# Nyström attention and a squared-ReLU feed-forward layer on one core: the order table searched anew, with other costs for late loads, adding transfers and GpSimd's additions

## The chip, the core and the metric

The kernel runs on one core of a Trainium2 chip. A core has five instruction queues that run side by side: TensorE (PE), VectorE (DVE), ScalarE (ACT), GpSimd (POOL) and SyncE (SP), and 16 DMA engines that carry transfers between the chip's memory and the core. Each queue works in order, so an instruction that waits holds all that stand behind it on its queue. The metric is the time of one execution in microseconds (us) of device time, as the median of several runs.

## What is computed

Two layers stand behind one another. The attention has 8 batches of 8 heads, 576 tokens and 64 features a head, with 32 landmarks (means of 18 neighbouring tokens); the feed-forward layer has 4608 tokens, 512 inputs and 2048 hidden units.

```python
q_lm = q.reshape(B, H, m, S // m, D).mean(axis=3)      # m = 32 landmarks
k_lm = k.reshape(B, H, m, S // m, D).mean(axis=3)
A, Bm, C = sm(q, k_lm), sm(q_lm, k_lm), sm(q_lm, k)    # softmax of the scaled products
Z = Bm.T / (norm1(Bm) * norminf(Bm) + 1e-6)
for _ in range(6):
    Z = 2 * Z - Z @ Bm @ Z
attn = A @ Z @ C @ v
x = attn.transpose(0, 2, 1, 3).reshape(B * S, H * D)
out = (np.maximum(x @ w_in, 0) ** 2) @ w_out           # float32
```

## The kernel before

The eight batches go through the core one behind another, and the stages of neighbouring batches are interleaved so that TensorE always has matrix products to do. Each piece of work is an *op* with a name; a number behind the name is the batch. The ops that matter here are, in the order in which one batch needs them:

- `ldq`, `ldk`, `ldv`: transfers of q, k and v, cast to bf16 on the way, issued on GpSimd's queue (L429, L455). `lx3` to `lx5` load q and k of batches 3 to 5 a second time in another layout, into the tile `XS` (L435).
- landmarks: matmuls of the loaded tile for batches 0 to 5 (`lm`, L500 from `XS`). For batches 6 and 7 the sums over tokens come from *adding transfers* (`la`, L443): for each of q and k of each of the two batches, three transfers go to the same 384 KB of `XS`, which is free again once the landmarks of batch 5 are done (`lm5`). The first of the three writes, the other two add (`accum_op`), and each of these has to wait until the one before it has landed. `la6.12` is batch 6, k, the third. Two additions of halves follow for each batch (`lma6.0` for q, `lma6.1` for k, L510), then two more (`lmc`, L514), a scaling (`lme`) and a transpose (`lmt`).
- `T` (L484): transposes of q and k on VectorE. `B`, `Bmx` to `Brn`: the 32 by 32 softmax and its column sums; `Bad` (L670) is a tiny addition in that chain, `Brn` its reciprocal. `N` and `U`: the six steps of Z on TensorE and VectorE, with `bd` (L679) laying out the next step's factor. `SS`: scores of A and C in two halves, `SS4.0` and `SS4.1` for batch 4. `At`, `Amx`, `Asb`, `Aex`, `Asu`, `Arc`, `Aml`, `Ab`: the softmax of A, and `Cmx`, `Cex`, `Crc`, `Cnr`, `CT`: that of C. `CV`, `Zm`, `ZC` and `W`: the products that fold v, Z and w_in into one weight for the batch (`We`).
- `F` (L1111): the first feed-forward product, `R` (L1132 on ScalarE, L1134 on VectorE) its ReLU out of PSUM, `Q` (L1139, L1141) the square into the tile `G`. `O` (L1158): the second product, `Oe` its copy out of PSUM, `St` its store. `F`, `R` and `Q` of batch 0 and 1 work on tokens in two parts.

What stands where is not left to a scheduler at run time. A table of words, `ORDER`, lists all ops. A word gives the op, the PSUM bank after `@` and, after `/`, the engine (A, D or P) where it isn't the op's first. A planner walks the table with a duration for each op and a rate for the transfers, and each engine's queue then gets its ops by the planned starts. The planner's numbers thus decide nothing on the chip but the order. Those that the change touches are the rate of late transfers in bytes per us (`RATE["late"]`, L205), the weight of an adding transfer's bytes (`ADD_COST`, L1254) and GpSimd's times for `lma` and `lmc` (L510, L514). A pair of lines of the planner says that ops marked with `port` on VectorE and GpSimd follow one another:

```python
            if e in o.port:
                t = max(t, port)
```

GpSimd has eight semaphores for its transfers, used in turn, so that a ninth is issued only when the one eight places ahead has landed.

Of the kernel before, what the change touches and what calls it, by code (L numbers as in the profile page):

```python
# [265 lines left out]
def kernel(  # L266
# [207 lines left out]
    def attention(b):  # L474
# [32 lines left out]
        def landmarks_added():  # L507
            acc, ls, kS = ACC[i2], LS[:, 0, 0:256].rearrange("p (t r d) -> p t r d", t=2, d=D), ("LS", 0)
            for t in range(2):
                op(f"lma{b}.{t}", {"POOL": 0.9, "DVE": v_(384)}, lambda e, t=t: eng(e).tensor_tensor(  # L510
                    acc[:, t, :, 0:3], acc[:, t, :, 0:3], acc[:, t, :, 3:6], ALU.add),
                   R=[("ACC", i2, t)], W=[("ACC", i2, t)], port=("POOL", "DVE"))
# [783 lines left out]
Aml1.1/P lmc2.00 O1.2 U1.4 lmc2.01 Cex1.0 lme2.0 O0.2 lmt2.0 T2.00 lx3.0 B2@2 N1.5@5 O1.3 Bmx2
U1.5 Crc1 Bsb2 CT1.0 Bex2 O3.2 ldq5.0 Bsu2 Cmk1 Oe1.0 Brc2 CT1.1 Bml2 Ap1.1@6 St1 Btf2 ldk3.1
Btr2/A Bcs2 Zd1@3 CR1@1 Bct2 Ab1.1/A O3.3 bt2/D Bnm2 Bad2 CRe1 Brn2 T2.11 BBT2@5 Zi2/P CV1@6,1
Oe3.0 ldv2.10 Zm1 St3 O0.3 Yi2 CVe1.1/A CVe1.0 bd2.0 T2.01 ZC1@7 Ap1.0@2 Oe0.0/D ZCe1.0 N2.0@1
O2.0@4 Ab1.0/A ZCe1.1/D St0 U2.0 ldk4.1 bd2.1/D W1.2@5 W1.0@0 W1.1@2 We1.00 We1.01/D N2.1@7 O2.1  # L1300
We1.1 ldk5.0 U2.1 We1.2/D W1.3@0 ldv3.10 O2.2 We1.3 bd2.2 T3.00 F1.4@2 F1.0@6 R1.4/D F1.2@0 R1.0
# [12 lines left out]
ldv5.00 U3.1 ZCe2.0 ZCe2.1/D bd3.2/D O8.1 Bsb4 Asb3.1 Bex4 Oe7.0 Amx3.0 N3.2@7 Aex3.1 W2.0@2 St7
W2.2@0 W2.3@4 We2.0 Bsu4 U3.2 O8.2 bd3.3/D We2.2/D We2.3 N3.3@7 W2.1@2 O8.3 We2.1 Asb3.0 F2.3@4
U3.3 Oe8.0 Crc3.0 F2.2@0 Cnr3.0 R2.3 Brc4 St8 F2.1@2 Bml4/P R2.2 Btf4 F2.0@6 Q2.3 R2.1 F2.5@4
Q2.2 St4 R2.0 F2.7@0 Q2.1 Asu3.1 F2.10@2 R2.5 F2.6@6 bd3.4/D R2.7 CT3.1 F2.9@4 Q2.5 R2.6 Q2.7
lm5.0@1 R2.9 Q2.0 Q2.6/A N3.4@0 F2.4@6 Q2.9 la6.00 U3.4 F2.13@4 R2.10 bd3.5/D CT3.0 O9.0@0 lme5.0
R2.13/D ldv5.10 R2.4 F2.14@2 la7.00 Q2.10 Aex3.0 N3.5@1 F2.11@4 U3.5 R2.14 F2.8@6 Zm3.2 Zm3.3
Zm3.0 R2.11 Arc3.1 O10.0@1 Q2.4 Q2.14/A Aml3.1 O10.1 R2.8 Asu3.0 Q2.8/A F2.15@2 lmt5.0 Arc3.0  # L1320
Q2.11/A CV3@4,6 Aml3.0 O9.1 Q2.13 CVe3.0/A CVe3.1/A Zm3.1 Ab3.0 R2.15 F2.12@4 T5.01 la6.10 ZC3@6
O9.2 R2.12 Q2.15 ZCe3.0/D Btr4/A la6.01 Q2.12/A O10.2 ZCe3.1/D bt4/D Bcs4 T4.00 W3.3@6 ldv6.11
W3.0@2 Ab3.1 W3.2@4 We3.0 We3.3/D O9.3 We3.2 O10.3 Oe9.0/D la7.10 BBT4@6 Bct4 F3.0@2 Oe10.0 Bnm4
F3.1@4 Bad4 Brn4 R3.0 T4.11 St10 Zi4/P O12.0@7 la7.01 R3.1 Yi4 bd4.0/D F3.2@0 T4.01 Q3.1/A St9
N4.0@6 W3.1@2 R3.2 U4.0 B5@4 O12.1 bd4.1/D We3.1 Bmx5 T5.00 N4.1@6 F3.3@0 Bsb5 Q3.2/A U4.1 O12.2
bd4.2 Bex5 R3.3/D Q3.0/A F3.6@4 Bsu5 la6.02 Brc5 T4.10 F3.5@0 N4.2@6 F3.4@2 Q3.3 R3.5 U4.2 la6.11
O12.3 R3.6 bd4.3/D Q3.5 R3.4 Bml5 N4.3@6 F3.9@0 Btf5 U4.3 Oe12.0 F3.7@4 Bcs5 bd4.4 R3.9/D F3.13@2
St12 la7.11 Bct5 F3.10@6 Q3.9/A R3.7/D N4.4@0 O11.0@1 R3.13 Q3.6 U4.4 R3.10 Bnm5 O11.1 T5.10
bd4.5 Q3.4/A SS4.0@2,4,6 Q3.7 Q3.10/A Bad5 N4.5@0 O11.2 la7.02 Brn5 Btr5 U4.5 At4.0 O11.3 bt5
Amx4.0 SS4.1@6 Zi5/P Oe11.0 ldv4.11 O13.0@0 Cmx4.1 St11 Cmx4.0 O15.0@1 Cex4.1 At4.1 O15.1 Cex4.0  # L1330
Asb4.0 BBT5@6 F3.12@4 Zm4.0 Aex4.0 Yi5 F3.11@2 Zm4.3 Crc4.1 Amx4.1 F3.8@6 R3.11 la6.12 Asu4.0
# [80 lines left out]
```

## Time and profile before

| | |
|---|---|
| median of 3 runs | 259.1 us (259.07 to 259.11) |
| the profiled execution | 259.34 us, of which 257.6 us from the first to the last instruction |
| granted TensorE clock | 0.999 |
| busy share of the span | PE 96%, DVE 82%, ACT 68%, POOL 33% |
| DMA: GpSimd's queue (q0) and the stores' (q1) | 58.7% and 14.0% of 16 engines' span |

The profiled execution is 0.24 us longer than the median. Its times are from the first instruction on. A busy PE is not PE at its peak, since matmuls overlap; a gap between two groups of matmuls shows as an idle time with the engine or the transfer that ended it. In a list of waits, each row gives who waited (engine, tile, line), for whom, and three numbers: us in all, times, longest. In a row of a timeline stand the start, the duration, engine, line, operation and tiles.

### The profile page before, as it was taken

What the parts mean: (1) busy time and instruction counts of PE and PEld (TensorE: products, weight loads), DVE (VectorE), ACT (ScalarE), POOL (GpSimd) and SP (SyncE); (2) the same over time, 40 slices, a digit from 0 to 9 for tenths busy, and PEclk for the clock granted to TensorE, in tenths of its full rate; (3) what the DMA queues carried; (4) which work ended last, traced back from release to release, by engine and by line L of the source; (5) the groups of instructions that cost most, each with busy time, mean ns of one, the idle gap of its engine ahead of it and who ended that gap; (6) DMA issues with size and microseconds to landing.
All of it is one profiled execution on the core that took longest, in us unless ns stands there. A gap on an engine that the chain in (4) does not pass through costs nothing.

```text
span 257.6 us, 7492 instructions
## 1 busy us (share of the span) xinstructions
PE 247.5 (96%) x3043; PEld 138.1 (54%) x3043; DVE 212.5 (82%) x553; ACT 175.6 (68%) x324; POOL 85.1 (33%) x137
## 2 busy tenths in 40 slices
PE   6999989999999989999999999999999999999993
PEld 2565554557464566565553565456454565467442
DVE  2989999889999988999999999987989698877201
ACT  0834876567697799788686699699865879457220
POOL 8576845652535304348561540110100300000000
PEclk9999999999999999999999999999999999999999
DMA  5999999999999999799979794032104110051035
GB/s 99 209 190 204 206 209 207 208 240 227 224 225 209 223 230 283 164 194 181 196 138 205 192 156 94 3 80 46 43 21 104 43 42 0 3 124 42 10 67 129
DMA packets 24610, 36.53 MB, mean 142 GB/s; under 512 B 2560, under 2 KB 13632, under 8 KB 24576
## 3 DMA queue, kind: packets, MB, share of 16 engines
q0 software_dynamic: 18656, 26.61, 58.7%
q1 hardware_dynamic: 5760, 9.31, 14.0%
q8 instruction: 24, 0.39, 0.6%
q10 hardware_dynamic: 160, 0.13, 0.2%
q14 instruction: 10, 0.08, 0.1%
HBM read 48.50 MB, written 9.44 MB: 225 GB/s over the span
## 4 chain that ended last, share of the span: by engine, by line
PE 66%; DMA 15%; DVE 10%; POOL 3%; issue 2%; ACT 2%; DVEq 0%; POOLq 0%
PE ps L1158 38%; PE ps L1111 16%; DMA X<-in_q_dram 9%; DMA XS<-in_q_dram 6%; PE ps L935 3%; DVE RS L1134 2%; PE ps L864 2%; DVE G L1141 2%; POOL X L429 1%; PE ps L778 1%; ACT WP L416 1%; DVE sm L816 1%; PE ps L529 1%; PE ps L742 1%; DVE An L1081 1%
## 5 line engine op out<-in xcount | busy, mean ns | idle before, releaser
L1158 PE MATMUL ps<-w_out,G 128*128 128x512 bf16 (+1 forms) x592 | 138.3, 374 | 0.3 <-DVE RS L1134 0.3
L1158 PEld LDWEIGHTS <-G 128*128 128x128 bf16 x592 | 53.2, 98 | 53.9 <-issue 6.0
L1111 PE MATMUL ps<-AT,WP 128*128 128x288 bf16 (+2 forms) x512 | 71.2, 286 | 1.1 <-DVE RS L1134 0.8
L1132 ACT ACTIVATE RS<-ps 128x576 bf16<-128x576 f32 (+2 forms) x101 | 61.1, 651 | 10.5 <-PE ps L1111 5.0
L1111 PEld LDWEIGHTS <-WP 128*128 128x128 bf16 x512 | 48.5, 98 | 20.6 <-issue 2.5
L1139 ACT ACTIVATE G<-RS 128x576 bf16<-128x576 bf16 (+2 forms) x55 | 36.4, 686 | 2.1 <-DVE RS L1134 1.8
L416 ACT COPY OS<-ps 128x512 f32<-128x512 f32 (+1 forms) x32 | 18.3, 573 | 23.0 <-PE ps L1158 21.8
L1141 DVE TENSOR_TENSOR G<-RS 128x576 bf16<-128x576 bf16 (+2 forms) x71 | 30.1, 445 | 2.6 <-ACT RS L1132 2.0
L416 ACT CAST WP<-ps 128x1024 bf16<-128x1024 f32 (+1 forms) x25 | 23.5, 983 | 6.7 <-PE ps L935 6.5
L679 POOL TENSOR_TENSOR BD<-ST,blkb 128x256 bf16<-128x256 bf16 x15 | 10.8, 718 | 47.4 <-DVE ST L756 43.2
L1134 DVE TENSOR_SCALAR RS<-ps 128x576 bf16<-128x576 f32 (+2 forms) x27 | 20.4, 760 | 4.9 <-PE ps L1111 3.8
L484 DVE STREAM_TRANSPOSE TT<-X 128x576 uint32<-128x576 uint32 x32 | 24.3, 761 | 0.0
L819 ACT ACTIVATE C<-ps,sm 128x576 bf16<-128x576 f32 x16 | 14.2, 902 | 7.7 <-DVE sm L816 7.7
L756 DVE SCALAR_TENSOR_TENSOR ST<-ST,ps 128x128 bf16<-128x128 bf16 (+1 forms) x48 | 12.8, 266 | 5.9 <-PE ps L742 3.6
L455 POOL DMA_DIRECT2D V<-in_v_dram x24 | 14.5, 603 | 6.2 <-DMA X<-in_q_dram 2.6
L420 DVE COPY OS<-ps 128x512 f32<-128x512 f32 x5 | 3.4, 675 | 12.3 <-PE ps L1158 12.3
L816 DVE TENSOR_REDUCE sm<-ps 128x1 f32<-128x576 f32 x16 | 11.5, 747 | 1.2 <-PE ps L778 1.1
L1236 PE MATMUL ps<-onesb 128*128 128x512 bf16 (+1 forms) x36 | 10.6, 392 | 1.6 <-DVE onesb L352 1.6
L420 DVE CAST WP<-ps 128x1024 bf16<-128x1024 f32 (+1 forms) x9 | 9.9, 1100 | 1.8 <-PE ps L935 1.7
L429 POOL DMA_DIRECT2D X<-in_q_dram x16 | 9.8, 642 | 4.1 <-PE ps L1111 2.2
L429 POOL DMA_DIRECT2D X<-in_k_dram x16 | 9.7, 607 | 3.6 <-DMA X<-in_k_dram 1.3
L1081 DVE TENSOR_TENSOR An<-SA,smA 128x640 bf16<-128x640 f32 (+1 forms) x12 | 10.3, 864 | 0.1
(151 smaller groups left out, 307.5 us busy)
## 6 DMA issues: line engine op xcount, KB each, us to landing
...
X<-in_k_dram POOLq DMA_DIRECT2D x16, 288.0 KB, 11.7
X<-in_q_dram POOLq DMA_DIRECT2D x16, 288.0 KB, 11.0
V<-in_v_dram POOLq DMA_DIRECT2D x8, 288.0 KB, 11.8
XS<-in_q_dram POOLq DMA_DIRECT2D x6, 384.0 KB, 6.5
XS<-in_k_dram POOLq DMA_DIRECT2D x6, 384.0 KB, 7.1
...
```

The costliest lines, as they stand in the source:

```text
L416: nc.scalar.copy(o, i)
L429: lambda e: nc.gpsimd.dma_start(x[:, t, r].rearrange("p s d -> p (s d)"), src),
L455: lambda e, r=r, p0=p0, n=n, src=src: nc.gpsimd.dma_start(vv[32 * p0:32 * (p0 + n), r].rearrange("p s d -> p (s d)"), src),
L484: op(f"T{b}.{t}{r}", {"DVE": v_(576) + 0.02}, lambda e, r=r: nc.vector.transpose(tt[:, t, r].rearrange("p s m e -> p (s m e)").bitcast(U32 ...
L816: op(f"Cmx{b}.{r}", {"DVE": v_(576)}, lambda e, r=r: nc.vector.tensor_reduce(s_[:, 12 + r:13 + r], cbanks(r), axis=AX.XY, op=ALU.max, nega ...
L819: op(f"Cex{b}.{r}", {"ACT": a_(576) + 0.27}, lambda e, r=r: nc.scalar.activation(Cs[r][:].rearrange("p x u -> p u x"), cbanks(r), AF.Exp, ...
L1111: nc.tensor.matmul(ps[:, ph.at + i, 0:w], lhsT=wp[:, r, 128 * ff:128 * ff + 128], rhs=at[:, r, t0:t0 + w], start=(r == 0), stop=(r == 1))
L1132: nc.scalar.activation(rs, pair(ph, w), AF.Relu)
L1134: nc.vector.tensor_scalar(out=rs, in0=pair(ph, w), scalar1=0.0, scalar2=None, op0=ALU.max)
L1139: nc.scalar.activation(g, rs, AF.Square)
L1141: eng(e).tensor_tensor(g, rs, rs, ALU.mult)
L1158: nc.tensor.matmul(bank(po)[:, 0:c1 - c0], lhsT=G[:, f, lo:lo + P], rhs=w_out[:, f, c0:c1], start=(f == 0), stop=(f == NF - 1))
```

## The change

Four numbers of the planner are set anew, and the table behind the shared beginning is another. The first 60 TensorE ops with the first rows of the other queues stay as they are, up to the column sums of batch 1's B (`Bcs1`) and some ops behind them; all that follows stands in another sequence, in part in other banks and on other engines. No product, sum or transfer is added or removed.

```diff
-RATE = {"sw": 0.375e6, "hw": 0.2e6, "first": 0.385e6, "then": 0.4e6, "late": 0.385e6}
+RATE = {"sw": 0.375e6, "hw": 0.2e6, "first": 0.385e6, "then": 0.4e6, "late": 0.355e6}
...
-                op(f"lma{b}.{t}", {"POOL": 0.9, "DVE": v_(384)}, lambda e, t=t: eng(e).tensor_tensor(
+                op(f"lma{b}.{t}", {"POOL": 1.5, "DVE": v_(384)}, lambda e, t=t: eng(e).tensor_tensor(
...
-                op(f"lmc{b}.0{j}", {"DVE": v_(256), "POOL": 0.65}, lambda e, j=j: eng(e).tensor_tensor(
+                op(f"lmc{b}.0{j}", {"DVE": v_(256), "POOL": 1.0}, lambda e, j=j: eng(e).tensor_tensor(
...
-ADD_COST = 1.5
+ADD_COST = 0.5
...
-R0.20/D R0.2 F0.18@4 R0.0 Q0.2 W0.2@6 Bad1 F0.22@2 R0.18/D We0.2 Q0.0/P F0.16@0 Brn1 R0.22/D
...
+R0.20/D R0.2 F0.18@4 R0.0 Q0.2 W0.2@6 Bad1 F0.22@2 R0.18/D We0.2 ldv1.00 F0.16@0 Brn1 R0.22/D c18
+Q0.0/A F0.12@4 F0.14@6 Zi1 Aex1.0 Btr1 R0.16/D O1.0@3 Q0.20/P Q0.22/A R0.14 BBT1@2 F0.30@0 Yi1
```

Of the table three lines are shown; the rest of it is told by the queues that come of it.

Three places of the queues matter most. In the rows below, a number behind a tile's name tells its buffers apart.

The first is GpSimd's queue just behind the shared beginning, before:

```order
L470 DMA w_out<-in_moe_w_out_dram 128x4x512 x2
L1141 TENSOR_TENSOR G<-RS_125 128x2x256
L455 DMA V_66<-in_v_dram 128x1152
L368 AFFINE_SELECT seg<-onesb 96x32
L370 AFFINE_SELECT seg<-seg 96x32
L455 DMA V_66<-in_v_dram 96x1152
```

and now:

```order
L470 DMA w_out<-in_moe_w_out_dram 128x4x512 x2
L455 DMA V_66<-in_v_dram 128x1152
L368 AFFINE_SELECT seg<-onesb 96x32
L370 AFFINE_SELECT seg<-seg 96x32
L1141 TENSOR_TENSOR G<-RS_127 128x2x320
L1141 TENSOR_TENSOR G<-RS_126 128x2x320
L429 DMA X_62<-in_k_dram 128x1152
L455 DMA V_66<-in_v_dram 96x1152
L1141 TENSOR_TENSOR G<-RS_128 128x2x320
L1141 TENSOR_TENSOR G<-RS_125 128x2x256
L1141 TENSOR_TENSOR G<-RS_126 128x2x256
```

The square `Q0.0`, the first L1141 of before, has gone to ScalarE's queue, and five other squares of batch 0 stand on GpSimd's (`Q0.20`, `Q0.18`, `Q0.30`, `Q0.8`, `Q0.10`) where `Q0.30` alone was left before; the ReLU `R0.16` goes from ScalarE to VectorE.

The second is GpSimd's queue where the adding transfers (L443) begin, before:

```order
L429 DMA X_63<-in_k_dram 128x1152
L429 DMA X_63<-in_q_dram 128x1152
L455 DMA V_67<-in_v_dram 128x1152
L619 TENSOR_TENSOR Bf_104<-Bl_102,sm_117 128x64
L443 DMA XS<-in_q_dram 128x2x384
L455 DMA V_67<-in_v_dram 96x1152
```

and now:

```order
L429 DMA X_63<-in_k_dram 128x1152
L429 DMA X_62<-in_q_dram 128x1152
L679 TENSOR_TENSOR BD_100<-ST_0_98,blkb 128x256
L679 TENSOR_TENSOR BD_101<-ST_1_99,blkb 128x256
L443 DMA XS<-in_q_dram 128x2x384 x2
L455 DMA V_67<-in_v_dram 32x1152
L443 DMA XS<-in_k_dram 128x2x384
```

Fewer loads are ahead of the first of them than before (35.96 MB as the table counts bytes, against 37.14 MB), and the loads of batch 5's second layout (`lx5`) stand further ahead, as the 32.42nd MB in place of the 34.78th. From there to the last adding transfer of batch 6, `la6.12`, the queue now holds `la6.00`, `la7.00`, a small part of v, `la6.10`, `la6.01`, `la6.11`, `la6.02`, `la7.10`, `ldk6.0`, `ldk5.1`, `la7.11`, `la7.01`, `ldk7.0`, `la7.12`, `ldq6.0` and `la6.12`: three first transfers of a sum ahead of the adding ones, and one among them; seven adding ones; four loads of q or k.

The third is VectorE's queue at batch 6's additions of halves (L510). Before, they stood behind batch 4's last step and its transposes (L1084), among the transposes of batches 5 and 6 (L484):

```order
L756 SCALAR_TENSOR_TENSOR ST_0_98<-ST_1_99,ps 128x128
L484 STREAM_TRANSPOSE TT_69<-X_64 128x576
L1084 STREAM_TRANSPOSE AT_81<-An_79 128x2x128
L679 TENSOR_TENSOR BD_100<-ST_0_98,blkb 128x256
L484 STREAM_TRANSPOSE TT_68<-X_62 128x576
L510 TENSOR_TENSOR XS<-XS 128x2x192
L420 CAST WP_94<-ps 128x2x512
```

Now the one of k, `lma6.1`, stands here:

```order
L703 TENSOR_TENSOR ST_0_98<-ps,sm_118 128x2x32
L679 TENSOR_TENSOR BD_100<-ST_0_98,blkb 128x256
L898 TENSOR_TENSOR ZM_86<-ST_0_96,blk_138 64x128
L816 TENSOR_REDUCE sm_117<-ps 128x1
L700 TENSOR_TENSOR ST_0_98<-Bf_105,sm_118 128x2x32
L1064 STREAM_TRANSPOSE SA_77<-ps 128x256 x2
L510 TENSOR_TENSOR XS<-XS 128x2x192
L830 RECIPROCAL sm_117<-sm_117 128x1
L422 TENSOR_SCALAR C_84<-C_84,sm_117 128x576
L756 SCALAR_TENSOR_TENSOR ST_1_99<-ST_0_98,ps 128x128
```

It has moved ahead, to the transposes of batch 4's second half of scores (L1064), and the row behind it with L756 is `U5.0`, the first step of Z for batch 5. The additions of batch 7, which stood on GpSimd, are on VectorE now: `lma7.1` right behind that `U5.0`, ahead of the layout `bd5.1` (L679) that batch 5's second step needs, and `lma7.0` later.

More of the change, by code (lines that the diff above doesn't have):

```diff
@@ L1296 @@
[L1296 to L1301, printed above, removed]
@@ L1314 @@
[L1314 to L1319, printed above, removed]
@@ L1320 @@
[L1320 to L1331, printed above, removed]
@@ new lines @@
+Cex4.0 Brn5 Yi5 bd5.0/D St10 Zm4.3 O13.0@1 Q3.13/A Cmx4.1 ldv5.10 Zi5 ldv5.00 Cex4.1 F3.11@2
+At4.1 St12 O13.1 ldq7.1 lma6.1/D R3.11 ldq7.0 Crc4.1 N5.0@6 Cnr4.1 F3.15@4 Q3.11/A U5.0 ldv6.00
+lma7.1/D F3.8@2 R3.15 bd5.1/D O14.0@7 CT4.1 R3.8 Asb4.0 N5.1@4 O14.1 Crc4.0 Q3.8 Aex4.0 Zm4.0
+F3.14@5 U5.1 bd5.2/D F3.12@2 Cnr4.0 R3.14 N5.2@4 O13.2 R3.12 U5.2 CT4.0 Q3.15/A O14.2 lmc6.00
+Zm4.2 Zm4.1 Q3.14/A Amx4.1 CV4@2,5 Q3.12/A Asb4.1 O15.2 CVe4.1 Aex4.1 Asu4.0 lmc6.01/P O15.3
+CVe4.0/A Arc4.0 Asu4.1 bd5.3 ZC4@5 O13.3 Oe15.0 ZCe4.0/D ldv7.11 lme6.0 ZCe4.1/D St15 N5.3@4
@@ L1377 @@
+O34.0@4 Q7.7 St30 Q7.13 O32.0@2 R7.11 R7.12/D Q7.11/A O35.5 F7.15@0 O35.6 R7.15/D O31.0@3 Q7.12
+O34.1 Q7.15 O34.2 O35.7 O31.1 Oe35.2 St35.4 O32.1 O32.2 O32.3 O31.2 Oe32.0 O34.3 St32 O31.3
+Oe34.0 O33.0@2 St34 Oe31.0 O33.1 St35.3 O33.2 St31 O33.3 O35.0@6 Oe33.0 O35.1 O35.2 St33 O35.3
+Oe35.0 St35.2 St35.1
 """
```

147 lines of the change are left out of this document (80 added, 67 removed).

## The prediction

> **What bounds the kernel now.** I read the busy shares first, then the list of TensorE's waits, then the timeline around the longest of them, and last the transfers. Shares and slices (a digit is the busy share of 6.4 us in tenths):
>
> ```profile
> PE 247.5 (96%) x3043; PEld 138.1 (54%) x3043; DVE 212.5 (82%) x553; ACT 175.6 (68%) x324; POOL 85.1 (33%) x137
> PE   6999989999999989999999999999999999999993
> DVE  2989999889999988999999999987989698877201
> DMA  5999999999999999799979794032104110051035
> ```
>
> TensorE works without a break from the first slice on; VectorE is nearly as full up to about 200 us, and the DMA engines are up to about 97 us. So the time is TensorE's work and the waits in it, and whatever is late on VectorE or in the transfers turns into such a wait. The waits of TensorE:
>
> ```profile
> PE ps L1236 <- DVE onesb L352: 1.6, 1, 1.6
> PE ps L1111 <- DVE RS L1134: 0.8, 1, 0.8
> PE ps L500 <- DMA XS<-in_q_dram: 0.7, 1, 0.7
> PE ps L1158 <- DVE RS L1134: 0.3, 1, 0.3
> PE ps L911 <- DVE CV L420: 0.2, 1, 0.2
> PE ps L911 <- DVE ZM L898: 0.2, 1, 0.2
> ```
>
> The first lies in the shared beginning. The other five, 2.2 us together, are what a new order can win in whole waits. The reader is to see how little that is: a change that moves nothing but the order has 1% of the time ahead of it, and a single new wait on VectorE can cost as much.
>
> **The first wait, 0.8 us, and Q0.0.** VectorE and GpSimd at that place, and the spread of line 670:
>
> ```profile
> 31.82 1.13 DVE L670 TENSOR_SCALAR sm<-sm 128x2 f32<-128x2 f32 x1
> 32.86 0.81 DVE L1134 TENSOR_SCALAR RS<-ps 128x640 bf16<-128x640 f32 x1
> 31.86 1.05 POOL L1141 TENSOR_TENSOR G<-RS 128x512 bf16<-128x512 bf16 x1
> L670 DVE TENSOR_SCALAR sm<-sm x7: 169/170/1131, 31.8 to 188.1; 128x2 f32<-128x2 f32 x7
> ```
>
> `Bad1` on two numbers takes 1.13 us in place of 0.17, for as long as GpSimd squares `Q0.0`; the ReLU behind it (`R0.18`) then frees a bank late, and `F0.12` waits. With `Q0.0` on ScalarE nothing on GpSimd stands beside `Bad1`, and 0.8 us goes. ScalarE pays one square, about 0.64 us, beside its 32% of idle time, and loses `R0.16` to VectorE (about 0.8 us); `F0.30`, which takes that bank, follows by TensorE's own work some 2.5 us behind `F0.16`, and VectorE's chain of two ReLUs, a transpose and `R0.16` just fills that, so 0 to 0.2 us is late next. I take −0.8 (bounds −0.95 and 0).
>
> Beside it: the Trainium skill, "SBUF — State Buffer", section "Who interferes with whom", says that VectorE and GpSimd share one pair of ports as an exclusive lock, held for the whole instruction. This row agrees (1.13 us against 0.17).
>
> Five squares of batch 0 stand on GpSimd now, where two did, and a square of 640 takes 1.27 us there:
>
> ```profile
> L1141 POOL TENSOR_TENSOR G<-RS x2: 1052/1158/1265, 31.9 to 39.8; 128x512 bf16<-128x512 bf16 x1, 128x640 bf16<-128x640 bf16 x1
> 135.40 0.99 DVE L898 TENSOR_TENSOR ZM<-ST,blk 64x128 bf16<-64x128 bf16 x1
> 134.79 1.51 POOL L510 TENSOR_TENSOR XS<-XS 128x384 f32<-128x384 f32 x1
> L898 DVE TENSOR_TENSOR ZM<-ST,blk x24: 202/220/994, 71.0 to 220.8; 64x128 bf16<-64x128 bf16 x24
> ```
>
> The last three rows are a second hold of the same kind: a `Zm` of 0.22 us takes 0.99 beside GpSimd's addition of halves, and gives the two waits of L911, 0.4 us. Those additions are on VectorE now (0.53 us each), so −0.4. Against it I set new holds: of two squares on GpSimd one cost TensorE 0.8 us, the other nothing; three more squares at 0.4 each would cost 1.2, but the table's `port` rule places most of them, so I take +0.4 (bounds 0 and +1.2). The wait of L1158, 0.3 us, comes of a like hold of a `Cnr` by a `bd`; such pairs are drawn anew, so it counts 0.
>
> **The landmarks of batch 5, 0.7 us.** The chain of work at that place, and the last loads ahead of the first adding transfers, by start:
>
> ```profile
> 80.79 15.54 DMA XS<-in_q_dram
> 96.46 0.84 PE ps L500 x24
> 84.64 0.59 POOL L429 DMA_DIRECT2D X<-in_k_dram  x1
> 87.44 0.53 POOL L455 DMA_DIRECT2D V<-in_v_dram  x1 [1.67 <-DMA X<-in_q_dram]
> ```
>
> and their times from issue to landing, in the same order of loads (k, then v):
>
> ```profile
> X<-in_k_dram POOLq DMA_DIRECT2D x1, 288.0 KB, 15.8
> V<-in_v_dram POOLq DMA_DIRECT2D x1, 288.0 KB, 16.0
> ```
>
> `lx5` lands at 80.79 + 15.54 = 96.3 us and `lm5` starts then. It now stands 2.36 MB further ahead in a queue that is never empty. The loads between (k at 84.64 + 15.8 = 100.4, a q, v at 87.44 + 16.0 = 103.4) land 1.5 us apart, 0.59 MB each, so that is 6 us sooner, at about 90, against a start of `lm5` at about 95. −0.7 (bounds −0.75 and 0).
>
> **The adding transfers, where a wait is new.** Their issues and landings:
>
> ```profile
> 97.61 0.75 POOL L443 DMA_DIRECT2D XS<-in_q_dram  x1 [4.96 <-PE ps L742]
> 112.18 1.23 POOL L443 DMA_DIRECT2D XS<-in_q_dram  x1 [0.96 <-issue]
> XS<-in_q_dram POOLq DMA_DIRECT2D x1, 384.0 KB, 5.8
> 123.70 1.25 POOL L443 DMA_DIRECT2D XS<-in_k_dram  x1
> XS<-in_k_dram POOLq DMA_DIRECT2D x1, 384.0 KB, 7.5
> q0 software_dynamic: 1587, 2.38, 96.2%
> ```
>
> The fourth and sixth rows' transfers are `la7.01` and `la6.12`: they land at 112.18 + 5.8 = 118.0 and 123.70 + 7.5 = 131.2. Between them stand four more adding transfers and a small part of v (0.4 us), so five land in 12.8 us: 2.56 us each, with GpSimd's queue alone taking 96% of the 16 engines from 117 to 132 us (the last row). A first transfer of a sum is cheap beside that: the one issued at 97.61 and the ones behind it land at 104.9 to 107.4, some 0.9 us each.
>
> Now the new queue. Its loads ahead of the first `la` end two loads sooner than those of before, at 103.4 − 2 × 1.5 = 100.4 us. Three first transfers and a small v: 3 × 0.9 + 0.4 = 3.1, so 103.5. From there to `la6.12`: seven adding ones at 2.56 (17.9), one first (0.9), four loads at 1.5 (6.0): it lands at 103.5 + 24.8 = 128.3 us. Before, it landed at 131.2, and nobody looked for it until 139.1 (the additions of halves).
>
> VectorE reaches `lma6.1` sooner than that. From the order and these rows:
>
> ```profile
> 124.11 1.42 DVE L816 TENSOR_REDUCE sm<-ps 128x1 f32<-128x576 f32 x2 [0.31 <-PE ps L778]
> 125.45 0.77 DVE L1064 STREAM_TRANSPOSE SA<-ps 128x256 f32<-128x256 f32 x2
> L510 DVE TENSOR_TENSOR XS<-XS x2: 517/532/548, 140.9 to 142.9; 128x384 f32<-128x384 f32 x2
> L510 DVEq EVENT_SEMAPHORE  x1: 21/21/21, 139.1 to 139.1; - x1
> ```
>
> The first row is what follows the second half of batch 4's scores, at 124.1. The same products of TensorE are ahead of it (0.2 us more), less 1.5 us of waits: 122.8. Behind it now stand two `Cmx` (0.71 each by the row), the pair of `At` (0.77), and between them `Bad5`, `Brn5`, `Yi5`, `bd5.0`, a `Zm` and `Zi5`, some 0.2 to 0.3 each, 1.4 together: `lma6.1` is due at 126.4 and stands until 128.3. Behind it are `Crc`, `Cnr`, `U5.0`, `lma7.1` and `bd5.1`, 2.4 us with its own 0.53, and then TensorE's `N5.1`, due by its own work 6.3 us behind the scores (five groups of four O at 0.86, three F at 0.49, some small ones), at 128.5. It starts at 130.7 in place of 128.5: +2.2. TensorE can do nothing else meanwhile, since its queue is in order. At an adding cost of 2.2 us the transfer lands at 125.8 and only 0.3 is left (VectorE's own length); with loads that end 2 us later the wait is 4.2. Bounds +0.3 and +4.2; I take 2.2, by the 2.56 of the fullest stretch. `la6.02` for `lma6.0` lands by the same count at 111.5, VectorE comes at 113: 0, by a margin of 1.5.
>
> In a sentence by itself: the Trainium skill, "DMA: Bandwidth & Descriptors", section "Anatomy of one DMA — SWDGE (gpsimd) path", fits a transfer at 2.0 us plus its bytes over 436e3 per us, which by its figures (an estimate) makes 0.9 us of an adding 384 KB in a full queue, so `la6.12` would land near 117 and the sum would be 2.2 us lower. The trace has 2.56 us, and I go by that.
>
> **The rest.** TensorE changes its tiling shape four times more behind the shared part (97 for 93); a group of four O ahead of such a change takes longer in the chain by 0.1 us, yet other short ops are saved one:
>
> ```profile
> 98.44 0.86 PE ps L1158 x4
> 103.80 0.97 PE ps L1158 x4
> ```
>
> +0.2 (bounds 0 and +0.4). Three two-input ops leave GpSimd and seven ops come to ScalarE, some 4.6 us beside 82 us of idle: 0; were that cover gone, a ReLU would be late by its 0.65. The loads of `lx3` and `lx4` land within 0.5 us of their landmarks, as before: 0 (up to +0.5 each). The end (the last O, its copy and two stores) has the same sequence: 0.
>
> **Sum.** 259.34 − 0.8 − 0.4 + 0.4 − 0.7 + 2.2 + 0.2 = 260.2 for the profiled execution; less the 0.24 by which it lies above the median, 260.0 us.
>
> **Rivals.** (a) The adding transfers are in time. Then the last step's own 0.3 is left of 2.2: 258.1, and with no new hold 257.7. For it speak the first transfers at 0.9 us and a lone adding transfer that lands within 5 us; against it the 96% of the engines. It decides at 2.2 us an adding transfer. The skill's fit above is a case of it. (b) A wide square on GpSimd holds VectorE in batch 0 and 1, with the wait of the adding transfers beside it: five squares at 1.05 to 1.27 us, each able to take up to 0.8 from TensorE; at three, +2.0 over the forecast: 262.0. For it speaks one hold in two squares, against it that VectorE's reads from PSUM (`R`, `U`, the reductions) ran at full speed beside the other. It decides when a `Q`, `Zi` or `bd` of VectorE falls under a square. (c) The gains are as told and the DVE wait is 1 us: 258.8, about no change.
>
> **How the numbers follow.** A measurement of this kernel tells 0.2% (0.5 us) from no change. Forecast (wait of about 2 us; 258.9 to 261.3): 0.45, of it 0.38 slower, 0.04 the same, 0.03 faster. (a), 256.6 to 258.5: 0.33, faster. (b), 261 to 264: 0.16, slower. (c): 0.06, of it 0.05 the same, 0.01 faster. Together faster 0.37, the same 0.09, slower 0.54. The range from 257.2 to 262.6 leaves out the lower end of (a), with no hold and no late load, and the upper end of (b).
>
> **What the profile of the changed kernel would show.** `Bad1` at 0.17 us and no wait at `F0.12`; L500 of batch 5 with no transfer ahead of it; a wait of VectorE's queue at L510 near 126 us for `XS` and one of TensorE at L742 or L747 of batch 5's second step near 128. Wrong would be: L510 without a wait, adding transfers that land 1 to 2 us apart, or a TensorE wait of over 1 us at a place that isn't named here.

## The result, and the profile after

The changed kernel takes 267.12 us (265.70 to 268.30) against 259.11 us before (259.07 to 259.61): a ratio of 1.030, with a 95% interval of 1.027 to 1.033. It is 3% slower, and it lies above the whole range that was forecast. Its profiled execution took 266.59 us, 7.25 us more than the one before. Ratios leave out an execution that lies more than 1.5% above the shortest of its kernel, which is one of run 1 and one of run 9. The kernel before was measured again beside the runs below (medians of 258.98 to 259.36 us), and their ratios are to that.

Busy shares and slices of the page after:

```profile
PE 249.8 (94%) x3043; PEld 138.1 (52%) x3043; DVE 209.0 (79%) x549; ACT 181.0 (68%) x331; POOL 83.8 (32%) x134
...
PE   6998999999999999998749999999999999999993
...
DVE  2988986898999999977367999989897988966200
...
PEclk9999999999999999999968999999999999999999
```

A slice is 6.6 us; PEld is TensorE's load of weights, and PEclk its granted clock in tenths. Up to 119 us TensorE's slices read much as before; then VectorE falls to 3 tenths and TensorE to 4, and TensorE's granted clock drops for two slices. TensorE's waits after:

```profile
PE ps L742 <- DVE BD L679: 5.0, 1, 5.0
...
PE ps L689 <- POOL BD L679: 1.4, 1, 1.4
...
PE ps L1158 <- DVE SA L1064: 0.4, 1, 0.4
...
PE ps L1111 <- ACT RS L1132: 0.3, 1, 0.3
```

The waits at L1111 for VectorE (0.8), at L500 (0.7) and the two at L911 (0.2 each) of before are not in the list any more. In their place stand 5.0 us at L742, batch 5's second step of Z (`N5.1`), and 1.4 us at L689, where the first step starts from `bt5` (`BBT5`).

The timeline around them: GpSimd's row of `bt5`, VectorE's rows from the scores' transposes to `bd5.1`, and TensorE's rows.

```profile
123.55 1.69 POOL L443 DMA_DIRECT2D XS<-in_k_dram  x1
124.30 1.64 POOL L679 TENSOR_TENSOR BD<-Bt,blkb 128x256 bf16<-128x256 bf16 x1
...
127.95 0.77 DVE L1064 STREAM_TRANSPOSE SA<-ps 128x256 f32<-128x256 f32 x2
134.26 0.56 DVE L510 TENSOR_TENSOR XS<-XS 128x384 f32<-128x384 f32 x1 [5.55 <-DMA XS<-in_k_dram]
...
135.88 0.28 DVE L679 TENSOR_TENSOR BD<-ST,blkb 128x256 bf16<-128x256 bf16 x1
...
125.99 0.21 PE L689 MATMUL ps<-Bt,BD 128*128 128x32 bf16 x2 [1.42 <-POOL BD L679]
...
136.22 0.29 PE L742 MATMUL ps<-ST,BD 128*128 128x64 bf16 x2 [5.03 <-DVE BD L679]
```

The reader is to see one chain: the first row issues the transfer `la6.12`; VectorE stands at L510 (`lma6.1`) for 5.55 us until it lands; `bd5.1` is behind that, and TensorE's `N5.1` behind `bd5.1`. Ahead of it, GpSimd does `bt5` only once it has issued `la6.12`, and takes 1.64 us for it.

Three windows of the same profile. Behind the stretch and its length stand the busy times of PE, PEld, DVE, ACT and POOL (with the number of instructions), then TensorE's granted clock, the DMA share (which can pass 1) and GB/s:

```profile
130.00:136.20 6.20, 1.20 (x7) 0.42 (x5) 1.90 (x7) 1.26 (x3) 1.59 (x3) 0.84 1.13 248
136.20:141.00 4.80, 4.78 (x19) 2.41 (x20) 3.11 (x11) 2.21 (x4) 0.00 (x0) 0.50 1.12 208
141.00:146.00 5.00, 5.00 (x98) 2.59 (x97) 4.84 (x11) 3.33 (x7) 1.92 (x3) 1.00 0.78 141
```

Behind the wait TensorE is busy for 4.78 of 4.80 us, but at half its clock: that loses 4.80 × 0.50 = 2.4 us. The balance of the profiled execution: 1.9 us of waits gone, 5.0 + 1.4 + 0.3 + 0.1 come, and 2.4 us of clock, together +7.3, against 7.25 measured.

### The profile page after: what moved, and what is told of

The parts are those of the page before. It is cut to its first block, busy times and chain, and to the rows that moved or that the text cites. A ratio compares the mean times of both kernels' runs of the same rounds, so it can differ in the third digit from the quotient of the medians.

```text
span 264.9 us, 7495 instructions
## 1 busy us (share of the span) xinstructions
PE 249.8 (94%) x3043; PEld 138.1 (52%) x3043; DVE 209.0 (79%) x549; ACT 181.0 (68%) x331; POOL 83.8 (32%) x134
## 4 chain that ended last, share of the span: by engine, by line
PE 69%; DMA 20%; POOL 5%; issue 3%; DVE 1%; ACT 1%; POOLq 0%
PE ps L1158 41%; PE ps L1111 18%; DMA XS<-in_k_dram 9%; DMA X<-in_q_dram 4%; DMA XS<-in_q_dram 4%; DMA w_out<-in_moe_w_out_dram 4%; PE ps L935 3%; PE ps L864 2%; POOL X L429 1%; PE ps L778 1%; POOL w_in L463 1%; PE ps L742 1%; PE ps L500 1%; POOL XS L443 1%; POOL G L1141 0%
## 5 line engine op out<-in xcount | busy, mean ns | idle before, releaser
L1158 PE MATMUL ps<-w_out,G 128*128 128x512 bf16 (+1 forms) x592 | 140.0, 376 | 0.4 <-DVE SA L1064 0.4
L1158 PEld LDWEIGHTS <-G 128*128 128x128 bf16 x592 | 54.1, 98 | 54.0 <-issue 6.4
L1111 PE MATMUL ps<-AT,WP 128*128 128x288 bf16 (+2 forms) x512 | 73.3, 289 | 0.5 <-ACT RS L1132 0.3
L1132 ACT ACTIVATE RS<-ps 128x576 bf16<-128x576 f32 (+2 forms) x103 | 63.4, 651 | 12.0 <-PE ps L1111 6.3
L1111 PEld LDWEIGHTS <-WP 128*128 128x128 bf16 x512 | 48.0, 98 | 20.1 <-issue 3.0
L1139 ACT ACTIVATE G<-RS 128x576 bf16<-128x576 bf16 (+2 forms) x61 | 40.1, 678 | 1.0 <-DVE RS L1134 0.4
L1141 DVE TENSOR_TENSOR G<-RS 128x576 bf16<-128x576 bf16 (+2 forms) x62 | 28.0, 463 | 2.7 <-ACT RS L1132 2.3
L416 ACT CAST WP<-ps 128x1024 bf16<-128x1024 f32 (+1 forms) x27 | 25.5, 989 | 5.3 <-PE ps L935 5.0
L679 POOL TENSOR_TENSOR BD<-ST,blkb 128x256 bf16<-128x256 bf16 x13 | 9.2, 709 | 53.7 <-DVE ST L756 53.7
L484 DVE STREAM_TRANSPOSE TT<-X 128x576 uint32<-128x576 uint32 x32 | 24.1, 754 | 0.0
L756 DVE SCALAR_TENSOR_TENSOR ST<-ST,ps 128x128 bf16<-128x128 bf16 (+1 forms) x48 | 12.8, 267 | 8.5 <-PE ps L742 5.3
L1073 ACT ACTIVATE SA<-SA 128x640 f32<-128x640 f32 (+1 forms) x12 | 8.3, 688 | 9.8 <-DVE SA L1071 9.8
L742 PE MATMUL ps<-ST,BD 128*128 128x64 bf16 (+1 forms) x72 | 8.1, 194 | 5.0 <-DVE BD L679 5.0
L742 PEld LDWEIGHTS <-BD 128*128 128x128 bf16 x72 | 6.5, 99 | 11.9 <-DVE BD L679 5.7
L429 POOL DMA_DIRECT2D X<-in_k_dram x16 | 11.8, 769 | 1.8 <-POOLq L1396 0.8
```

The source lines that it names most:

```text
L416: nc.scalar.copy(o, i)
L429: lambda e: nc.gpsimd.dma_start(x[:, t, r].rearrange("p s d -> p (s d)"), src),
L484: op(f"T{b}.{t}{r}", {"DVE": v_(576) + 0.02}, lambda e, r=r: nc.vector.transpose(tt[:, t, r].rearrange("p s m e -> p (s m e)").bitcast(U32 ...
L742: nc.tensor.matmul(bank(pN)[:, w * r:w * r + w], lhsT=BD[it % 2][:, r, :], rhs=av[:, lo:64], start=True, stop=True)
L1111: nc.tensor.matmul(ps[:, ph.at + i, 0:w], lhsT=wp[:, r, 128 * ff:128 * ff + 128], rhs=at[:, r, t0:t0 + w], start=(r == 0), stop=(r == 1))
L1132: nc.scalar.activation(rs, pair(ph, w), AF.Relu)
```

## The experiments

The theory after these traces has three parts. A: VectorE's wait for `la6.12` holds `N5.1`. B: `bt5` is late because GpSimd's queue issues adding transfers ahead of it. C: TensorE's clock, which drops in the wait, costs more behind it. The rival to A and B is that VectorE's own order or the wide squares on GpSimd are slow and the transfers only come last; to C, that the slow products have another cause. The diffs below are fragments of the order table. The four numbers of the planner need no run: with their old values under the new table every queue is word for word the same, so they act through the table alone.

**Run 1: the additions of halves late.**

```diff
-At4.1 St12 O13.1 ldq7.1 lma6.1/D R3.11 ldq7.0 Crc4.1 N5.0@6 Cnr4.1 F3.15@4 Q3.11/A U5.0 ldv6.00
-lma7.1/D F3.8@2 R3.15 bd5.1/D
+At4.1 St12 O13.1 ldq7.1 R3.11 ldq7.0 Crc4.1 N5.0@6 Cnr4.1 F3.15@4 Q3.11/A U5.0 ldv6.00
+F3.8@2 R3.15 bd5.1/D
...
+Ab4.1 lma6.1/D lmc6.00 We4.1 W4.2@6 F4.0@0 We4.2 O16.2
+T5.11 lmc6.01/P lme6.0 lmt6.0 lma7.1/D lma7.0/D lmc7.00 T6.10 O16.3
```

> The kernel after, with VectorE's additions of halves for batches 6 and 7 and what hangs on them moved behind batch 4's transposes (the additions of k of batch 6 behind Ab4.1, the rest behind T5.11): VectorE no longer stands for the transfer la6.12 ahead of U5.0 and bd5.1. Theory A (that wait holds N5.1 for 5.2 us, and the half clock behind it costs 2.2 us more): the wait of line 742 goes, the clock stays up, and the time falls from 267.1 to about 259.7, with BBT5's wait of 1.4 us for GpSimd still there. Rival (VectorE is late there by its own work and the new squares on GpSimd, the transfer only shows as the last): N5.1 still waits 3 us or more and the time stays above 264.

Measured: 263.37 us (261.60 to 265.94), 1.015 of before (1.008 to 1.021); without the longest execution the median is 262.55. The wait at L742 is gone, so the rival to A falls, but some 3 us more than expected are left. TensorE's waits of this run:

```profile
PE ps L773 <- DVE ST L756: 1.7, 1, 1.7
...
PE ps L689 <- POOL BD L679: 1.1, 1, 1.1
```

The second is `BBT5`. The first is new: the additions, `lmc` and `T6.10` stood in one block on VectorE ahead of `U5.4`, and the scores of batch 5 waited for that.

**Run 2: `bt5` on VectorE.**

```diff
-Btf5 U4.5 Q3.4/A ldq6.0 Q3.7 Bcs5 Oe12.0 la6.12 SS4.0@2,4,6 Bct5 Bnm5 O11.2 Btr5/A At4.0 bt5
+Btf5 U4.5 Q3.4/A ldq6.0 Q3.7 Bcs5 Oe12.0 la6.12 SS4.0@2,4,6 Bct5 Bnm5 O11.2 Btr5/A At4.0 bt5/D
```

> The kernel after, with bt5 alone taken from GpSimd, where it stands behind the adding transfers, to VectorE. Theory B (bt5 waits behind the transfers that GpSimd's queue issues, and is a wait of its own): BBT5's 1.4 us goes, yet N5.1 still waits for the landing of la6.12, so the time stays within 0.5 us of 267.1 and the wait of line 742 grows by about 1.4 us, to 6.4. Rival (the two waits add up): 265.6, with line 742 still at 5.0.

Measured: 267.16 us (265.85 to 269.58), as after. `BBT5` waits no more, and L742 takes over:

```profile
PE ps L742 <- DVE BD L679: 5.9, 1, 5.9
```

So the landing is a fixed point: what is won ahead of it is waited off there. B is a wait of its own only when A is mended.

**Run 3: both.** The edits of runs 1 and 2 together.

> Both edits in one kernel: the additions of halves late and bt5 on VectorE. Theories A and B together: neither wait, the clock up throughout, 267.1 - 5.2 - 2.2 - 1.6 = 258.1, 1 us below the kernel before, since the waits of the shared part that the change took away stay away. Rival (the new order costs something of its own at other places too): above 259.5.

Measured: 262.19 us (260.95 to 263.20), 1.012 of before (1.007 to 1.016): 5 us of the 8, and a miss of 4 us against the sum. The wait of 1.7 us at L773 is there again. The windows around it:

```profile
143.00:146.00 3.00, 1.24 (x67) 0.66 (x65) 2.90 (x7) 1.17 (x2) 1.33 (x3) 1.00 1.07 293
146.00:150.00 4.00, 3.41 (x32) 1.38 (x11) 3.22 (x7) 1.79 (x4) 0.56 (x1) 0.57 0.50 96
```

Behind the wait the clock was 0.57 for four us, which cost another 1.5 us of the 3.41 that TensorE was busy. The wait was not all that went before: from 143 to 146 us TensorE was busy for 1.24 of 3.00 us, nearly all of it with the small products (32 by 32) of batch 5's scores. These are sizes of the profiled execution, which took 260.95 us; two others took 263.2, and what they lost more isn't shown.

**Run 4: `la6.12` sooner.** VectorE's queue stays as it is; the transfer goes ahead of `la7.10` and what follows.

```diff
-W3.3@4 BBT4@3 Ab3.1 O9.3 Yi4 T5.01 We3.3 la6.02 F3.2@2 bd4.0/D
+W3.3@4 BBT4@3 Ab3.1 O9.3 Yi4 T5.01 We3.3 la6.02 la6.12 F3.2@2 bd4.0/D
...
-Bcs5 Oe12.0 la6.12 SS4.0@2,4,6
+Bcs5 Oe12.0 SS4.0@2,4,6
```

> The kernel after, with the transfer la6.12 issued right behind la6.02, ahead of la7.10, four loads and the adding transfers of batch 7; VectorE's queue is the same word for word. Theory A (the landing of the transfer sets N5.1): la6.12 lands near 118 us, lma6.1 finds it there, and the next in line, lma7.1, waits for la7.12, which is pushed back by one adding transfer to about 130.8; N5.1 starts near 133 in place of 136.2 and the time is 262 to 264.5. Rival (VectorE's own order sets N5.1): 267, no change.

Measured: 265.04 us (264.38 to 265.76), 0.5 us above the upper end of A's range and 2 us below the rival's 267. The wait at L742 is gone, since `lma6.1` finds its data. But `BBT5` waits 3.9 us in place of 1.4, and GpSimd's rows show why:

```profile
125.82 1.18 POOL L443 DMA_DIRECT2D XS<-in_k_dram  x1 [3.49 <-DMA XS<-in_k_dram]
126.54 1.05 POOL L429 DMA_DIRECT2D X<-in_q_dram  x1
127.13 1.16 POOL L679 TENSOR_TENSOR BD<-Bt,blkb 128x256 bf16<-128x256 bf16 x1
```

GpSimd's queue stands 3.49 us for the landing that `la7.12` has to wait for, and `bt5` (the third row) stands behind it. That is B at its plainest.

**Run 9: run 4, and `bt5` on VectorE.**

> As the fourth run (la6.12 issued right behind la6.02), and bt5 on VectorE. In the fourth run the wait of line 742 had gone and BBT5 waited 3.9 us for bt5 on GpSimd, whose queue stood for batch 7's adding transfers. If bt5's place is the whole of what was left: that wait goes, and then lma7.1 is looked for at about 128.5 with la7.12 landing near 131, so N5.1 waits some 2 us again: 262 to 263.5. Rival (nothing else is late there): 259.5 to 260.5.

Measured: 264.58 us (263.14 to 267.46), 1.019 of before (1.015 to 1.023); without the longest execution the median is 263.48, at the upper end of what was expected. The next in line, `lma7.1`, is indeed late. The profile is of the longest of the four executions, so its sizes don't hold for the others. VectorE's row in its timeline:

```profile
136.09 0.56 DVE L510 TENSOR_TENSOR XS<-XS 128x384 f32<-128x384 f32 x1 [6.32 <-DMA V<-in_v_dram]
```

and the transfer `la7.12`, issued at 128.07, with its us to landing:

```profile
XS<-in_k_dram POOLq DMA_DIRECT2D x1, 384.0 KB, 7.9
```

The row puts the wait down to a transfer of v; the adding one landed at 128.07 + 7.9 = 136.0, when VectorE went on. Whichever sum comes last, an addition that VectorE reaches at 128.7 us (in after) or 129.8 us (here) comes too early for it.

**Run 5: the price of adding.**

```diff
-                    accum_op=ALU.add if j else ALU.bypass),
+                    accum_op=ALU.bypass),
```

> The kernel after with the adding transfers replaced by plain ones: same bytes, same tiles, same order and waits, but each transfer overwrites instead of adding, so the landmark sums of batches 6 and 7 are left out and the output differs there. Theory A with its price (an adding 384 KB takes 2.3 to 2.6 us of a full queue, a plain one 0.9): the seven adding ones ahead of la6.12 and itself save about 1.5 us each, la6.12 lands 8 to 12 us sooner, near 124, VectorE finds it there, N5.1 and BBT5 wait for nothing, and the time falls to 258 to 259.5. Rival (these transfers are slow for their shape or their waits for one another, not for the addition): la6.12 still lands behind 131 and the time stays above 265.

This kernel leaves out the additions of the landmark sums of batches 6 and 7. Measured: 258.11 us (257.53 to 259.35), 0.996 of before (0.994 to 0.998). All of the loss goes with the addition alone: same bytes, same tiles, same queues, same waits for one another. GpSimd's issues of k's sums (ns of the shortest, the median and the longest), after:

```profile
L443 POOL DMA_DIRECT2D XS<-in_k_dram x6: 761/1224/1685, 98.3 to 123.5; - x6
```

and in this run:

```profile
L443 POOL DMA_DIRECT2D XS<-in_k_dram x6: 709/729/753, 99.7 to 121.1; - x6
```

A window of the same stretch (the last two columns are the DMA share and GB/s), after:

```profile
104.00:112.00 8.00, 8.00 (x74) 4.03 (x73) 7.93 (x22) 7.68 (x12) 4.81 (x6) 1.00 0.87 132
```

and in this run:

```profile
104.00:112.00 8.00, 7.95 (x77) 3.93 (x76) 7.91 (x20) 7.67 (x13) 3.79 (x6) 1.00 0.61 178
```

And this run's timeline, with `bt5` on GpSimd, VectorE's transposes of the scores and `lma6.1`:

```profile
123.07 0.66 POOL L679 TENSOR_TENSOR BD<-Bt,blkb 128x256 bf16<-128x256 bf16 x1 [1.20 <-ACT Bt L416]
...
128.05 0.77 DVE L1064 STREAM_TRANSPOSE SA<-ps 128x256 f32<-128x256 f32 x2
128.74 0.52 DVE L510 TENSOR_TENSOR XS<-XS 128x384 f32<-128x384 f32 x1
```

With the addition the DMA engines are busier and move less: 0.87 for 132 GB/s against 0.61 for 178. An issue is recorded with 1.22 us on GpSimd in place of 0.73, and `bt5` with 1.64 in place of 0.66; in after these spans overlap one another, so they are rough. `lma6.1` at 128.74 follows its predecessor at once. One thing I missed: I had `la6.12` at 124 without the addition. GpSimd's row at 128.32, the load eight places behind it, waits 0.65 us for it, so it landed near 128, only just ahead of VectorE. The waits of the transfers for one another keep the queue slow even then: from issue to landing `la6.01`, `la6.02`, `la7.11`, `la7.01` and `la7.12` took 4.1, 4.0, 4.5, 5.0 and 5.6 us, against 5.3, 5.0, 5.1, 6.6 and 6.0 in after, so what adding costs here is 0.4 to 1.6 us at each step of a chain.

**Run 6: TensorE kept busy in the wait.**

```diff
-Asb4.0 N5.1@4 O14.1
+Asb4.0 fx@5 N5.1@4 O14.1
...
+        for _ in range(24):
+            nc.tensor.matmul(bank(px), lhsT=onesb[:, 0:P], rhs=onesb[:], start=True, stop=True)
```

> The kernel after with 24 dummy products of 512 columns, 5.2 us, on a bank of their own ahead of N5.1, which adds work that no output uses: TensorE is busy while it would wait. Theory C (the 2.2 us lost between 136 and 141 us come from TensorE's clock, which drops to half after the idle time): the clock stays near 1 and the time falls to about 265, though nothing of the wait goes. Rival (the slow products behind the wait have another cause, transfers or VectorE's reads): the time stays at 267 or rises.

Measured: 264.10 us (263.21 to 264.72), 3.0 us less than after, by adding 5.3 us of work. TensorE's rows in its timeline, and VectorE's at `lma6.1`:

```profile
129.78 5.34 PE L1218 MATMUL ps<-onesb 128*128 128x512 bf16 x23
135.31 0.23 PE L742 MATMUL ps<-ST,BD 128*128 128x64 bf16 x2 [0.18 <-DVE BD L679]
...
133.35 0.56 DVE L510 TENSOR_TENSOR XS<-XS 128x384 f32<-128x384 f32 x1 [5.81 <-DMA XS<-in_k_dram]
```

and two windows:

```profile
130.00:136.00 6.00, 5.76 (x28) 2.52 (x28) 2.62 (x8) 0.11 (x1) 1.59 (x3) 1.00 1.12 249
136.00:141.00 5.00, 4.74 (x95) 2.63 (x95) 4.83 (x15) 3.53 (x6) 1.90 (x3) 1.00 1.12 212
```

VectorE still stands for `la6.12`, and `N5.1` starts when `bd5.1` is there, but the clock stays at 1.00. So C is shown. Its size is not the whole 3.0 us: `la6.12` landed 0.9 us sooner in this profile (133.35 against 134.26), and `N5.1` started 0.9 us sooner with it (135.31 against 136.22). From `N5.1` to the last instruction this run takes 126.8 us and after 128.7, so the clock is worth 1.9 us by this profile, near the 2.2 that I had put on it.

The Trainium skill, "TensorE: Matmul & The Clock Gate", section "Part 1: The HAM clock gate (the "warmup" mystery)", says that TensorE's clock falls to half behind an idle window of about 3.4 us and comes back behind a busy one. The rows of after agree (0.50 behind a wait of 5.0 us, 1.00 again 4.8 us later). Run 3's are not told by the longest wait: it was 1.7 us, in a stretch of small products, and the clock fell to 0.57. A wait of 2.06 us in run 8, below, stood behind wide products (L1158), and the clock didn't fall. So a stretch without a wait of 3.4 us can lose the clock too, but the length of its longest wait doesn't decide it; whether the small products do isn't shown.

**Run 8: VectorE's late work spread.**

```diff
-T5.11 lmc6.01/P lme6.0 lmt6.0 lma7.1/D lma7.0/D lmc7.00 T6.10 O16.3 R4.0 lmc7.01/P T6.00
+T5.11 lmc6.01/P lme6.0 lma7.1/D lma7.0/D lmc7.00 lmt6.0 O16.3 R4.0 lmc7.01/P
...
+U5.5 T6.10
...
+Amx5.0 T6.00
```

> As the third run (the additions of halves late, bt5 on VectorE), but the late VectorE work is spread so that U5.4 isn't behind it: lmt6.0 behind lma7.1, lma7.0 and lmc7.00, the transposes T6.10 and T6.00 behind U5.5 and Amx5.0; and lma6.0 one step later, behind bd4.3. In the third run SS5.1 waited 1.7 us for U5.4 and the clock was at 0.66 in the 5 us around it. If that wait and the clock behind it were what kept it at 262.2 against the 258.1 expected: 258.0 to 259.0. Rival (the order has a cost of its own elsewhere, or a wait moves to the next place): above 260.

Measured: 259.79 us (259.02 to 260.73), 1.002 of before (1.000 to 1.004): 2.4 us better than run 3, but above the expected 258.0 to 259.0, and short of the rival's 260. The wait at L773 is gone and another stands elsewhere. TensorE's granted clock by slices, its row in the timeline, and GpSimd's issue of `ldv4.11`:

```profile
PEclk9999999999999999999999999999999999999998
...
135.32 0.82 PE L864 MATMUL ps<-V,CT 32*64 32x128 bf16 x72 [2.06 <-ACT SA L1073]
...
125.07 1.52 POOL L455 DMA_DIRECT2D V<-in_v_dram  x1
```

and that transfer's us to landing:

```profile
V<-in_v_dram POOLq DMA_DIRECT2D x1, 72.0 KB, 10.2
```

The wait of `CV4` is put down to ScalarE, but 125.07 + 10.2 = 135.27 is when the last small part of batch 4's v landed, and `CV4` reads it.

**Run 12: one small transfer moved.** Run 8 with `ldv4.11` ahead of `la7.12` and `la6.12`; all other queues stay the same.

```diff
-ldk7.0 R3.4 N4.4@1
+ldk7.0 ldv4.11 R3.4 N4.4@1
```

> The kernel with the additions spread (259.8 us), with one edit: the transfer ldv4.11, 144 KB of batch 4's v, ahead of la7.12 and la6.12 in GpSimd's queue; every other queue is the same word for word. If the landing of this transfer, not ScalarE's softmax of A, made CV4 wait 2.1 us: the wait at line 864 goes and the time falls to about 257.8 to 258.3. Rival (ScalarE): no change, 259.8.

Measured: 258.67 us (258.50 to 261.51), 0.999 of before (0.997 to 1.001). The wait at L864 is gone, so it was the transfer. The time is 0.4 us above the expected range. The profiled execution, at 260.17 us one of the longer ones, shows GpSimd's queue once more:

```profile
138.23 0.23 PE L742 MATMUL ps<-ST,BD 128*128 128x64 bf16 x2 [1.21 <-POOL BD L679]
...
136.95 0.53 POOL L455 DMA_DIRECT2D V<-in_v_dram  x1 [2.95 <-DMA XS<-in_k_dram]
137.50 0.68 POOL L679 TENSOR_TENSOR BD<-ST,blkb 128x256 bf16<-128x256 bf16 x1
```

`bd5.3` on GpSimd stands behind a load that waits 2.95 us for an adding transfer. How much of this the median holds isn't shown.

**Run 10: all places mended.** Run 12's moves, with the additions of batch 7 on GpSimd and two transposes elsewhere.

```diff
-lma7.1/D lma7.0/D
+lma7.1/P lma7.0/P T6.10 lmt6.0
...
+Cmx5.0 lmc7.00 lmc7.01/P
...
+Brn6 T6.00
```

> The order of after mended at all places found so far: the additions of halves late, those of batch 7 on GpSimd as in the kernel before, T6.10 ahead of U5.4 and T6.00 behind Brn6, bt5 on VectorE, lma6.0 one step later, and ldv4.11, a small part of batch 4's v that stood behind la6.12 in GpSimd's queue, ahead of la7.12. In the run before CV4 waited 2.1 us, put down to ScalarE, while ldv4.11 landed at the moment when CV4 started. If that transfer is the cause: the wait at line 864 goes, and 259.8 - 2.1 = 257.7. Rival (ScalarE's softmax of A is the cause): the wait stays and the time is 259.5 or more.

Measured: 258.12 us (257.80 to 261.49), 0.9969 of before (0.9942 to 0.9996), 0.4 us above the expected 257.7. None of the waits in this chain is left; behind the beginning, the largest of TensorE's that another engine or a transfer ended are of 0.4 us, among them

```profile
PE ps L1111 <- ACT RS L1132: 0.4, 1, 0.4
```

This version beats both kernels, the one before by only 0.3%, with an interval that all but reaches no change.

**Run 7: the first step alone.** The kernel before with `Q0.0` on ScalarE.

```diff
-R0.20/D R0.2 F0.18@4 R0.0 Q0.2 W0.2@6 Bad1 F0.22@2 R0.18/D We0.2 Q0.0/P F0.16@0 Brn1 R0.22/D
+R0.20/D R0.2 F0.18@4 R0.0 Q0.2 W0.2@6 Bad1 F0.22@2 R0.18/D We0.2 Q0.0/A F0.16@0 Brn1 R0.22/D
```

> The kernel before with one word changed: Q0.0 on ScalarE in place of GpSimd. By the prediction's first step: Bad1 at 0.17 us, no wait at F0.12, and 259.0 - 0.8 = 258.2. Rival (a later wait takes the gain): 259.0.

Measured: 259.19 us (258.56 to 259.63), 0.9997 of before (0.998 to 1.001): no change, as the rival said. `Bad1` takes 0.16 us and the wait at L1111 is gone, so the step does what it says. This profile can't show where the gain went, since TensorE's granted clock fell to 0.75 between 24 and 28 us in it, for a reason that I can't tell; the pages of runs 5, 6 and 9 show it at 7 or 8 tenths in the slice at 26 to 33 us too.

**Run 11: the first step, and the landmarks' loads of batch 5 sooner.**

```diff
-lme4.0 O6.3 lx5.0 CT2.1
+lme4.0 O6.3 lx5.0 ldv4.00 ldv4.10 CT2.1
```

(the two transfers of v stood ahead of `lm4.0`; `Q0.0` as in run 7.)

> The kernel before with two edits: Q0.0 on ScalarE, and two transfers of batch 4's v (1.02 MB as the table counts) moved behind lx5.0, so that the landmarks' loads of batch 5 land about 2.5 us sooner. With Q0.0 alone the time did not fall: F0.12's wait went, yet lm5 started when lx5.0 landed, at 95.9 us against 96.3. If that landing takes up the gain, both together give 259.2 - 0.9 - 0.7 = 257.6. Rival (the first step's gain isn't there at all, or the moved loads make another wait): 258.6 or more.

Measured: 259.36 us (258.75 to 260.06), 1.000 of before (0.998 to 1.002): a miss of 1.8 us. What ended the idle time of line 500 (us, times), before:

```profile
  DMA XS<-in_q_dram: 1.0, 2
```

in this run:

```profile
  DMA XS<-in_q_dram: 2.7, 2
```

and the landmarks of batch 3 in this run's timeline:

```profile
61.63 0.84 PE L500 MATMUL ps<-XS,seg 96*32 96x256 bf16 x24 [1.23 <-DMA XS<-in_q_dram]
```

In this profile the 0.8 us of the first step is waited off at the next fixed point, which is the load of batch 3's landmarks and not, as I had thought, that of batch 5's: `lm3` starts at 61.63 us here and at 61.80 before. By this the step has a worth only in an order that brings these loads sooner as well. The changed kernel's does (the second of them is issued at 44.28 us, before at 47.38), and its line 500 waits for no transfer at all; that step by itself was not tried.

## Why the prediction was wrong

The forecast was 260.0 us with a range to 262.6; measured were 267.1. Point by point, in its own steps:

- *The first wait and `Q0.0`, −0.8*: right in the changed kernel. `Bad1` takes 0.16 us, the wait of 0.8 us at L1111 is gone, and one of 0.3 us for ScalarE's ReLU is there, near the 0 to 0.2 that was allowed. Runs 7 and 11 show that it isn't a gain by itself: by run 11's profile it needs the loads of batch 3's landmarks sooner, a condition that the sum doesn't have.
- *Five squares on GpSimd, +0.4, and the additions of halves off GpSimd, −0.4*: the two waits at L911 are gone, and no wait of over 0.4 us can be laid to a square. Rival (b) didn't come: with the adding chain mended run 10 stands at 258.1.
- *The landmarks of batch 5, −0.7*: right, L500 waits for no transfer.
- *The adding transfers, +2.2 with bounds of 0.3 and 4.2*: the step that failed. The place was right, VectorE's wait at `lma6.1` and `N5.1` behind it; the landing of `la6.12` was not. The count had `la6.10` at 103.5 and `la6.12` 24.8 us behind it, at 128.3. Five transfers of after by their us to landing, issued at 98.3, 108.18, 108.91, 122.25 and 123.55:

```profile
XS<-in_k_dram POOLq DMA_DIRECT2D x1, 384.0 KB, 5.4
...
XS<-in_q_dram POOLq DMA_DIRECT2D x1, 384.0 KB, 5.0
...
XS<-in_k_dram POOLq DMA_DIRECT2D x1, 384.0 KB, 6.9
...
XS<-in_k_dram POOLq DMA_DIRECT2D x1, 384.0 KB, 6.0
...
XS<-in_k_dram POOLq DMA_DIRECT2D x1, 384.0 KB, 10.7
```

  `la6.10` landed at 103.7, as counted. Then `la6.02`, the third adding one behind it, at 113.2: 9.5 us for three, where 3 × 2.56 = 7.7 were counted (+1.8). `la7.10`, a first transfer, at 115.8: 2.6 in place of 0.9 (+1.7). `la7.12`, with three adding ones and three loads, at 128.25: 12.4 against 12.2 (+0.2). `la6.12`, with one load, at 134.25: 6.0 against 4.1 (+1.9). Together 30.5 us in place of 24.8. The count let the transfers follow one another at the price of a full queue. GpSimd's issues of `la7.11` and `la7.12` show what happens in its place:

```profile
116.84 1.23 POOL L443 DMA_DIRECT2D XS<-in_k_dram  x1 [5.55 <-issue]
...
122.25 1.18 POOL L443 DMA_DIRECT2D XS<-in_k_dram  x1 [2.34 <-DMA XS<-in_k_dram]
```

  Each is issued only when the transfer ahead in its sum has landed (`la7.10` at 115.8, `la7.11` at 116.84 + 5.1 = 121.9), and `la6.12`, whose own sum was ready by 111, stands behind them in the queue. So the stretch is made of landings: 115.8, 1.0 to the next issue, 5.1, 0.3, 6.0 give the 128.25, and that 12.4 us lie beside the 12.2 of the count is luck. The engines were not full either: their share was 0.24 from 102 to 104 us, 0.49 from 106 to 108 and 0.68 from 118 to 120. The last 6.0 us lie in a full stretch (a share of 1.08 from 128 to 134 us), with the six transfers that GpSimd issued behind `la6.12` on their way as well. VectorE came 2.3 us later than the 126.4 of the count, at 128.7, 1.4 of it by `BBT5`. The wait of `N5.1` came out at 5.0 us, above the upper bound.
- *Two terms were not in the sum.* `bt5` on GpSimd behind the adding transfers: 1.4 us at `BBT5`. I followed what the moved transfers hold on VectorE's queue, but not what they hold on GpSimd's own, where that product stands. And the clock: 2.4 us by the windows of after, 1.9 by run 6's profile. The first is covered only by the prediction's last sentence, "a TensorE wait of over 1 us at a place that isn't named here"; the second by nothing in it.
- *The tiling shapes, +0.2*: not tried by itself; run 10 leaves room for no more.
- *Rival (a)*, transfers in time at 257.7 to 258.1, is what runs 5 and 10 are (258.11 and 258.12). Its point of decision, a price of 2.2 us an adding transfer, was the wrong measure: the landings that each issue waits for up to `la6.12` decide, and when VectorE looks for it.

The 0.9 us that the prediction worked out from the fit of the Trainium skill ("DMA: Bandwidth & Descriptors", section "Anatomy of one DMA — SWDGE (gpsimd) path"), an estimate, put `la6.12` near 117 us. The trace has 134.2, and without the addition still some 128, so it does not carry over to transfers that add or that wait for one another.

What stays open: why the clock fell between 24 and 28 us in run 7's profile, what besides the length of a wait brings it down, and how much of the last 6.0 us ahead of `la6.12`'s landing is due to the transfers issued behind it.
